# A fused retention and feed-forward kernel: one block of keys-values, one load, one store and the fill-in products of TensorE are moved or reshaped

## The chip, the cores and the metric

The kernel runs on one core of a Trainium2 chip. A core has five engines with instruction streams of their own: TensorE (in profiles PE for its products and PEld for its weight loads), VectorE (DVE), ScalarE (ACT), GpSimd (POOL) and SyncE (SP, which here issues nearly all DMAs). They meet at semaphores. The metric is the device time of one execution in microseconds; before the change it is 181.31 us, the median of three runs (181.07 to 181.83).

## The reference

Two parts follow one another. The first is retention over 4 batches, 8 heads, 768 tokens and head dimension 64: a state of 64 x 64 decays by a factor of its head, takes up the outer product of key and value, and is read by the query. The second is a feed-forward part over the 3072 x 512 result: two products with 512 x 1024 weights, multiplied with each other, then `w3` (1024 x 1024) and `w_out` (1024 x 512).

```
state = gamma * state + outer(k[t], v[t])
y[t]  = q[t] @ state / sqrt(64)
x     = y, heads side by side            # 3072 x 512
out   = ((x @ w1) * (x @ w2)) @ w3 @ w_out
```

Inputs and output are fp32.

## The kernel before

The tokens are worked in 12 steps of 256 (three per batch). Products run in fp16 with fp32 sums. `w3 @ w_out` is multiplied once, in the first 33 us, into eight tiles `W3O`, so that each step needs only three large products.

A step `n` has these parts. Queries, keys and values are loaded (`load`, line 82, or `fetch`, line 120, which is a load by name), cast to fp16 (`cast`, line 314; `cast_v`, line 331, also multiplies the values by a table of decays) and turned: queries and keys go head dimension first, for step 2 and 3 on TensorE (`turn`, line 361, with `turned`, line 374, as the copy out of the accumulator), from step 4 on by a transposing DMA (`dma_turn`, line 354). `scores` (line 390) multiplies keys by queries and `mask` (line 413) masks them on VectorE. `kv` (line 433) multiplies keys by values in small products of 64 rows, and `state` (line 466) adds them up, chunk by chunk, on VectorE (the last multiplication by the decay goes to GpSimd). `inter` and `av` (lines 498 and 534) bring query times state and scores times values into one accumulator, and `x_out` (line 556) writes the step's fp16 activations.

The feed-forward part of a step is four units `u`, each with a block `a` (with `w1`) and a block `b` (with `w2`). A block is eight products of 128 x 128 weights by 256 columns into one bank of the accumulator memory (`two_blocks`, line 578; `blk`, line 704). `evac` (line 707) takes it out: `a` by ScalarE as a copy, `b` by VectorE as the product with that copy. Then `o_unit` (line 636) multiplies with `W3O`, `o_copy` (line 660) copies to an output tile, and `o_store_all` (line 677) stores 512 KB.

The accumulator memory has eight banks, by name: `S0`, `S1`, `X0`, `X1`, `K`, `F0`, `F1`, `F2`. A bank is given again to its next user only when all work on the one before has ended; this holds also where TensorE follows TensorE. Blocks rotate over the three `F` banks.

The order of every engine's work is written out by hand (`tc.manual_schedule`, line 53): the list of calls from line 713 on is the order in which each engine gets its instructions. SyncE's list is in this order too, so a DMA that has to wait for its source holds up those behind it. Loads take a tile of a pool of 18 (`NSTAGE`, line 38).

`warm` (line 688) multiplies zeros into a bank that nobody reads. It is called between the first parts of the work, up to line 771, 18 products of 512 columns in all. Lines 987 to 1000 are what the change touches in step 3: `kv(3, ...)`, the copies and the states around the blocks of step 2. Lines 1001 to 1019 are the loads and turns of the steps 5 to 7. Line 1083 stores the outputs of step 2 (the third), whose tile comes from a rotation of three (`o_tile`, line 651). `YS` (line 197) is a table of decays for steps 0 and 1, last read by `x_out` at line 564. Lines 1178 to 1181 begin the blocks of step 6. Lines 1333 to 1335 are stores near the end.

Of the kernel before, what the change touches and what calls it, by code (L numbers as in the profile page):

```python
# [9 lines left out]
FP = mybir.dt.float32  # L10
# [10 lines left out]
def kernel(  # L21
# [11 lines left out]
    nc = tc.nc  # L33
    B, H, S, D = q.shape
    T = 256
# [5 lines left out]
    DM = 512  # L41
# [4 lines left out]
    const = ctx.enter_context(tc.tile_pool(name="const", bufs=1))  # L46
# [24 lines left out]
    def bank(tag, shape, dtype=FP):  # L71
        return psum.tile(shape, dtype, tag=tag, name="ps" + tag)
# [47 lines left out]
    def fetch(names, via=nc.sync):  # L120
        for x in names.split():
            kind, i = x[:-1], int(x[-1])
            if kind == "r":
                w3_st[i] = load_rows(moe_w3, i, via)
            elif kind == "wo":
                wo_st[i] = load_wo(i, via)
            elif kind in ("w1", "w2"):
                w_st[kind, i] = load_rows({"w1": moe_w1, "w2": moe_w2}[kind], i, via)
            else:
                load(kind, i)  # L130
# [302 lines left out]
    def kv(n, tags, parts=(0, 1)):  # L433
        last = n % PER == PER - 1
        assert kv_n.get(n, 0) == parts[0]
        kv_n[n] = parts[-1] + 1
        if 0 not in parts:
            pass
        elif n < EO:
            KB[n] = [bank(tags[g], [128, NP, 64]) for g in range(2)]  # L440
        else:
            KB[n] = [bank(tags[g], [128, 2, NP, 64]) for g in range(2)]
        for a in range(2 * parts[0], 2 * parts[-1] + 2):
            for t in range(2):
                for g, r in QUARTERS:
                    h = 2 * a + r
                    hd = slice(h * D, (h + 1) * D)
                    if n < EO:
                        o = KB[n][g][half(r), a, :]
                    elif last and (t, g) == (1, 1):  # L450
                        continue
                    else:
                        o = KB[n][g][half(r), t, a, :]
                    nc.tensor.matmul(
                        o, lhsT=k16[n][half(g), t, hd], rhs=v16[n][half(g), t, hd],
                        start=(a == 0 and t == 0), stop=(t == 1), skip_group_check=True,
                    )
# [117 lines left out]

    HT, pa, ht_n = {}, {}, {}

    def two_blocks(W, n, u, tag):
        need(*[(w, d, c) for w in ("w1", "w2") for d in range(4) for c in (0, 512)])
        assert x_n[n] == 2  # L580
        ps = bank(tag, [128, 2, T])
        for i in range(2):
            f = 2 * u + i
            for d in range(4):
                nc.tensor.matmul(  # L585
                    ps[:, i, :], lhsT=W[d][:, f * 128 : (f + 1) * 128], rhs=XT[n][:, d, :],
                    start=(i == 0 and d == 0), stop=(i == 1 and d == 3),
                )
        return ps

    def a_evac(n, u, ps, eng="s"):
# [57 lines left out]
    o_sb, o_n = {}, {}  # L649

    def o_tile(n, tb):
        if n < 2:
            if (n, tb) not in o_sb:
                o_sb[n, tb] = wpool.tile([128, DM], FP, tag=f"wo_{2 * n + tb}", name="osw")
            return o_sb[n, tb][:, :]
        if n not in o_sb:
            o_sb[n] = fsb.tile([128, 2, DM], FP, tag="osb", name="osb", bufs=3)
        return o_sb[n][:, tb, :]
# [26 lines left out]
            o_copy(n, tb, *c)  # L685
            o_store(n, tb, *c)

    def warm(m, tag="X1", w=512):
        ps = bank(tag, [128, 512])
        for _ in range(m):  # L690
            nc.tensor.matmul(ps[:, 0:w], lhsT=zeros[:, 0:128], rhs=zeros[:, 0:w], start=True, stop=True)

    def cast_w(W, st, d, eng, c0=0, c1=DFF):
        done.update((st, d, c) for c in range(c0, c1, 512))
# [6 lines left out]
    ab = {}  # L701
    cuts = ((0, 320), (320, 512))

    def blk(w, n, u, tag):
        ab[w, n, u] = two_blocks(W1 if w == "a" else W2, n, u, tag)

    def evac(w, n, u, eng="s"):
        if w == "a":
            a_evac(n, u, ab.pop((w, n, u)), eng)
        else:  # L710
            b_evac(n, u, ab.pop((w, n, u)))
# [33 lines left out]
    fetch("q3")  # L745
    identity()
    fetch("q4")
    warm(8)
    numbers()
    arguments()  # L750
    tables(4)
# [2 lines left out]
    tables(2)  # L754
    cast_w3(4, "v")
    turn_w3(4, "S0")
    warm(3, "F2")
    turned_w3(4, "v")
    step_decays()
    warm(2, "F2")  # L760
    cast_wo(0, "s")
    cast_w3(1, "v")
    keeps()
    warm(1, "F2")
    cast_w3(2, "gs")
    warm(1, "F2")
    turn_w3(1, "S1")
    tables(0)
    fetch("v3")
    turned_w3(1, "sv")  # L770
    warm(3, "F2")
    cast_wo(1, "g")
    turn_w3(2, "X0")
    w3_mm(1, 0, "S1", first=True)
# [209 lines left out]
    cast_v(4, "g")  # L984
    evac("a", 2, 0)
    blk("b", 2, 0, "F1")
    kv(3, ("X0", "K"))
    turned("q", 3, "v")
    state(3, 1)
    fetch("k5")  # L990
    fetch("v5")
    blk("b", 2, 1, "F0")
    state(3, 2)
    blk("a", 2, 1, "F2")
    state(3, 3)
    scores(3, ("S0", "S1"))
    o_copy(1, 1)
    evac("b", 2, 0)
    state(3, 4)
    state(3, 5)  # L1000
    fetch("k6")
    blk("a", 2, 2, "F1")
    fetch("q6")
    cast("q", 5, "g")
    evac("a", 2, 1)
    evac("b", 2, 1)
# [6 lines left out]
    blk("b", 2, 3, "F1")  # L1013
    inter(3, 0, ("X0", "X1"))
    dma_turn("q", 5)
    fetch("v6")
    mask(3, 0)
    fetch("k7")
# [61 lines left out]
    mask(5, 1)  # L1080
    load("k", 8)
    load("q", 8)
    o_store_all(2)
    o_unit(3, 0, ("F2",))
    o_copy(3, 0)
    o_unit(3, 1, ("F0",))
# [88 lines left out]
    o_copy(5, 0)  # L1175
    o_unit(5, 1, ("F0",), pieces=2)
    o_copy(5, 1)
    blk("a", 6, 0, "F2")
    evac("a", 6, 0)
    blk("b", 6, 0, "F0")  # L1180
    evac("b", 6, 0)
    blk("a", 6, 1, "F1")
    evac("a", 6, 1)
# [147 lines left out]
    x_out(10, 0)  # L1331
    x_out(10, 1)
    o_store_all(8)
    o_store(0, 0)
    o_store(0, 1)
    state(11, 1)
# [92 lines left out]
```

## Time and profile before

| | |
|---|---|
| median of three runs | 181.31 us (181.07 to 181.83) |
| the profiled execution | 181.6 us, span 179.9 us |
| TensorE clock granted, mean | 0.999 |
| TensorE busy | 173.4 us, 96% of the span |
| VectorE, ScalarE, GpSimd busy | 103.0, 66.1 and 63.6 us |
| DMA | 40.22 MB, mean 224 GB/s |
| the products of the blocks (L585) | 640 of 256 columns, 273 ns each from start to end |
| a store of 512 KB, issue to landing | 5.4 us (median) |

The span runs from the first to the last instruction. The duration of one product is from its start to its modelled end; products follow one another much closer than that. The page divides the span in 40 slices of about 4.5 us and gives tenths of busy time for each. The chain that ended last goes back from the last instruction to what released it, or to the instruction before it on the same engine. In rows of the order of time, the columns are start, length (both us), engine, line, operation, tiles written and read, shapes, and how many instructions were merged; square brackets hold the idle time before it and what ended it. The rows of waits give the engine, tile and line that waited, what it waited for, and us in total, times, and the longest.

### The profile page before, as it was taken

The numbers are of one execution on the slowest core, as the hardware profiler recorded it, in microseconds if no ns is written. First come the engines' busy times: TensorE is split into PE (matmuls) and PEld (weight loads), VectorE is DVE, ScalarE is ACT, GpSimd is POOL, SyncE is SP. The second block draws the span as 40 slices with busy tenths as digits, with TensorE's granted clock in tenths as the row PEclk, the third lists the DMA queues.
The fourth block names the chain that finished last, engine by engine and source line by source line (L and its number), as shares of the span: only waits on it lengthen the run. The fifth ranks groups of instructions, "written<-read, shape, count | busy, mean of one in ns | idle before, by whom it ended". The sixth has DMA issues, their size and how long they took to land.

```text
span 179.9 us, 6072 instructions
## 1 busy us (share of the span) xinstructions
PE 173.4 (96%) x2642; PEld 125.7 (70%) x2642; DVE 103.0 (57%) x177; ACT 66.1 (37%) x118; POOL 63.6 (35%) x93
## 2 busy tenths in 40 slices
PE   7989899999999999999999999999999999999993
PEld 2445456688956785885867898768688587786872
DVE  2342789883946487547366384474764946734330
ACT  5436537681238332323314314223222131232422
POOL 7753076446232742724445055250453200000000
PEclk9999999999999999999999999999999999999999
DMA  5999999999899899999999999999999552150303
GB/s 206 409 418 360 357 325 389 408 282 226 181 244 236 204 179 221 202 204 238 178 241 228 237 284 178 212 240 232 271 211 263 170 166 71 70 166 5 117 0 117
DMA packets 80025, 40.22 MB, mean 224 GB/s; under 512 B 59392, under 2 KB 73984, under 8 KB 80000
## 3 DMA queue, kind: packets, MB, share of 16 engines
q1 hardware_dynamic: 79856, 39.33, 88.6%
q8 instruction: 20, 0.33, 0.8%
q10 hardware_dynamic: 144, 0.52, 0.8%
q14 instruction: 5, 0.04, 0.1%
HBM read 29.36 MB, written 6.29 MB: 198 GB/s over the span
## 4 chain that ended last, share of the span: by engine, by line
PE 72%; DMA 15%; SPq 5%; POOL 3%; ACT 2%; DVE 1%; issue 1%; POOLq 0%; DVEq 0%
PE psF L585 38%; PE psF L643 20%; DMA st<-in_v_dram 8%; DMA st<-in_q_dram 4%; DMA st<-in_moe_w_dram 4%; SPq L112 3%; PE psX L521 2%; POOL v L69 2%; PE psX L548 2%; PE psS L406 1%; PE psK L299 1%; PE psF L299 1%; ACT pa L61 1%; SPq L89 1%; PE psF L621 1%; PE psX L621 1%
## 5 line engine op out<-in xcount | busy, mean ns | idle before, releaser
L585 PE MATMUL psF<-xt,w 128*128 128x256 f16 x640 | 71.9, 273 | 0.0
L585 PEld LDWEIGHTS <-w 128*128 128x128 f16 x640 | 62.4, 98 | 9.2
L69 DVE TENSOR_TENSOR ht<-pa,psF 128x512 f16<-128x512 f32 x43 | 29.4, 687 | 38.9 <-PE psF L585 38.8
L61 ACT COPY pa<-psF 128x512 f32<-128x512 f32 x43 | 25.2, 585 | 51.2 <-PE psF L585 45.6
L643 PE MATMUL psF<-w3o,ht 128*128 128x512 f16 (+3 forms) x200 | 38.4, 346 | 0.0
L643 PEld LDWEIGHTS <-ht 128*128 128x128 f16 x224 | 20.7, 98 | 17.5
L69 POOL TENSOR_TENSOR v<-st,VN 128x1024 f16<-128x1024 f32 x10 | 19.0, 1902 | 37.2 <-DMA st<-in_v_dram 18.5
L663 ACT ACTIVATE osb<-psF 128x512 f32<-128x512 f32 (+2 forms) x18 | 9.9, 550 | 31.0 <-PE psF L643 31.0
L566 DVE TENSOR_TENSOR xt<-psX,YN 128x512 f16<-128x512 f32 x19 | 12.8, 724 | 5.7 <-PE psX L548 5.7
L426 DVE TENSOR_TENSOR am<-psS,keep 128x512 f16<-128x512 f32 x19 | 12.5, 681 | 2.6 <-PE psF L406 2.6
L621 PEld LDWEIGHTS <-w 128*128 128x128 f16 x128 | 12.1, 98 | 2.4 <-issue 0.5
L61 POOL CAST q<-st 128x1024 f16<-128x1024 f32 x10 | 10.4, 1039 | 7.2 <-DMA st<-in_q_dram 4.3
L61 POOL CAST k<-st 128x1024 f16<-128x1024 f32 x9 | 9.3, 1036 | 6.2 <-PE psX L548 3.1
L299 PEld LDWEIGHTS <-w3t 128*128 128x128 f16 x64 | 5.8, 98 | 6.4 <-issue 0.7
L621 PE MATMUL psF<-xt,w 128*128 128x256 f16 x56 | 9.7, 272 | 0.0
L69 POOL TENSOR_TENSOR t<-s,GS 128x256 f16<-128x256 f32 x8 | 5.8, 727 | 11.0 <-DVE s L69 11.0
L521 PE MATMUL psX<-qT,t 64*64 64x64 f16 (+1 forms) x296 | 7.6, 199 | 0.0
L69 POOL TENSOR_TENSOR v<-st,VS 128x1024 f16<-128x1024 f32 x2 | 3.9, 1932 | 8.9 <-DMA st<-in_v_dram 8.9
L521 PEld LDWEIGHTS <-t 64*64 64x64 f16 x320 | 4.9, 106 | 3.0 <-issue 2.5
L69 DVE TENSOR_TENSOR t<-psK,t 128x256 f16<-128x256 f32 x15 | 6.2, 415 | 0.4
L283 PEld LDWEIGHTS <-w3h 128*128 128x128 f16 x64 | 4.2, 101 | 2.9 <-DVE w3h L61 1.4
L621 PE MATMUL psX<-xt,w 128*128 128x256 f16 x32 | 6.1, 273 | 0.1
(127 smaller groups left out, 192.4 us busy)
## 6 DMA issues: line engine op xcount, KB each, us to landing
st<-in_moe_w_dram SPq DMA_DIRECT2D x15, 512.0 KB, 8.7
st<-in_k_dram SPq DMA_DIRECT2D x20, 256.0 KB, 5.7
st<-in_q_dram SPq DMA_DIRECT2D x10, 512.0 KB, 6.1
st<-in_v_dram SPq DMA_DIRECT2D x20, 256.0 KB, 4.6
out_dram<-osb SPq DMA_DIRECT2D x9, 512.0 KB, 5.4
st<-in_moe_w_out_dram SPq DMA_DIRECT2D x4, 512.0 KB, 9.8
st<-in_k_dram SPq DMA_DIRECT2D x2, 512.0 KB, 6.5
st<-in_q_dram SPq DMA_DIRECT2D x8, 128.0 KB, 6.5
```

Of the source, the lines that this page charges most:

```text
L61: {"v": nc.vector.tensor_copy, "g": nc.gpsimd.tensor_copy, "s": nc.scalar.copy}[eng](dst, src)
L69: (nc.vector if eng == "v" else nc.gpsimd).tensor_tensor(dst, a, b, op)
L112: via.dma_start(t[:, :].rearrange("p (t n) -> p t n", t=2), moe_w_out[i * 256 : (i + 1) * 256, :].rearrange("(p t) n -> p t n", t=2),)
L283: nc.tensor.transpose(ps[:, g * 128 : (g + 1) * 128], src[:, c0 : c0 + 255 : 2], ident16[:, :])
L299: nc.tensor.matmul(acc[f][:, :], lhsT=w3t[f][:, g * 128 : (g + 1) * 128], rhs=WO[i][:, r, :], start=(first and r == 0), stop=(last and r = ...
L426: nc.vector.tensor_tensor(t[:, :, :, :].rearrange("p a s i -> p (a s) i"), ps[:, :, :, :].rearrange("p a s i -> p (a s) i"), keep64[:, :]. ...
L521: nc.tensor.matmul(dst, lhsT=TS[n, c][half(r), a, :], rhs=rhs, start=((g, o) not in begun), stop=False, skip_group_check=True,)
L566: nc.vector.tensor_tensor(XT[n][:, :, :].rearrange("p a (s x) -> p (a s) x", s=2)[:, :, g * 64 : (g + 1) * 64].rearrange("p k (i t) -> p k ...
L585: nc.tensor.matmul(ps[:, i, :], lhsT=W[d][:, f * 128 : (f + 1) * 128], rhs=XT[n][:, d, :], start=(i == 0 and d == 0), stop=(i == 1 and d = ...
L621: nc.tensor.matmul(rows_ps[w, n, uh][j // 2][:, j % 2, :], lhsT=W[d][:, f * 128 : (f + 1) * 128], rhs=XT[n][:, d, :], start=(first and j % ...
L643: nc.tensor.matmul(ps[:, x : x + w], lhsT=HT[n][:, f, tb * 128 : (tb + 1) * 128], rhs=W3O[f][:, c0 + x : c0 + x + w], start=(f == 0 and x ...
L663: nc.scalar.activation(dst, src, AF.Copy, scale=final_scale)
```

## The change

It has five parts.

- In step 3, `kv(3)` and the first `state` after it come behind block `b` of unit 1 rather than ahead of it, and the `evac` of block `b` of unit 0 comes ahead of the states.
- The load of the queries of step 6 is issued behind the two turns of step 5 rather than ahead of them.
- The outputs of step 2 go to a tile of their own, in the place of the table `YS`, and are stored near the end, behind the outputs of step 8.
- The products of zeros read the same zeros as fp32: eleven of 256 or 128 columns for 18 of 512. Each is one instruction of the program, where the fp16 ones were a weight load and a product.
- The blocks `a` and `b` of unit 0 in step 6 are multiplied in pieces of 128 columns: 32 products for 16.

```
-    def two_blocks(W, n, u, tag):
+    def two_blocks(W, n, u, tag, pieces=1):
...
             for d in range(4):
-                nc.tensor.matmul(
-                    ps[:, i, :], lhsT=W[d][:, f * 128 : (f + 1) * 128], rhs=XT[n][:, d, :],
-                    start=(i == 0 and d == 0), stop=(i == 1 and d == 3),
-                )
+                for x in range(0, T, T // pieces):
+                    nc.tensor.matmul(
+                        ps[:, i, x : x + T // pieces], lhsT=W[d][:, f * 128 : (f + 1) * 128],
+                        rhs=XT[n][:, d, x : x + T // pieces], start=(i == 0 and d == 0 and x == 0),
+                        stop=(i == 1 and d == 3), skip_group_check=pieces > 1,
+                    )
...
+        if n == 2 and n not in o_sb:
+            o_sb[n] = const.tile([128, 2, DM], FP, tag="YS", name="osy")
...
-    def warm(m, tag="X1", w=512):
-        ps = bank(tag, [128, 512])
+    def warm(m, tag="X1", w=256):
+        ps, z = bank(tag, [128, 512]), zeros[:, :].bitcast(FP)
         for _ in range(m):
-            nc.tensor.matmul(ps[:, 0:w], lhsT=zeros[:, 0:128], rhs=zeros[:, 0:w], start=True, stop=True)
+            nc.tensor.matmul(ps[:, 0:w], lhsT=z[:, 0:128], rhs=z[:, 0:w], start=True, stop=True)
...
-    warm(8)
+    warm(4)
...
     turn_w3(4, "S0")
-    warm(3, "F2")
+    warm(1, "F2")
+    warm(1, "F2", w=128)
     turned_w3(4, "v")
     step_decays()
-    warm(2, "F2")
+    warm(1, "F2")
     cast_wo(0, "s")
     cast_w3(1, "v")
     keeps()
-    warm(1, "F2")
+    warm(1, "F2", w=128)
     cast_w3(2, "gs")
-    warm(1, "F2")
+    warm(1, "F2", w=128)
     turn_w3(1, "S1")
     tables(0)
     fetch("v3")
     turned_w3(1, "sv")
-    warm(3, "F2")
+    warm(1, "F2")
+    warm(1, "F2", w=128)
...
     blk("b", 2, 0, "F1")
-    kv(3, ("X0", "K"))
     turned("q", 3, "v")
-    state(3, 1)
     fetch("k5")
     fetch("v5")
     blk("b", 2, 1, "F0")
+    kv(3, ("X0", "K"))
+    evac("b", 2, 0)
+    state(3, 1)
     state(3, 2)
     blk("a", 2, 1, "F2")
     state(3, 3)
     scores(3, ("S0", "S1"))
     o_copy(1, 1)
-    evac("b", 2, 0)
     state(3, 4)
     state(3, 5)
     fetch("k6")
     blk("a", 2, 2, "F1")
-    fetch("q6")
...
     dma_turn("q", 5)
+    fetch("q6")
     fetch("v6")
...
-    o_store_all(2)
...
-    blk("a", 6, 0, "F2")
+    blk("a", 6, 0, "F2", pieces=2)
     evac("a", 6, 0)
-    blk("b", 6, 0, "F0")
+    blk("b", 6, 0, "F0", pieces=2)
...
     o_store_all(8)
+    o_store_all(2)
     o_store(0, 0)
```

More of the change, by code (lines that the diff above doesn't have):

```diff
@@ L702, with blk @@
     cuts = ((0, 320), (320, 512))
-    def blk(w, n, u, tag):
-        ab[w, n, u] = two_blocks(W1 if w == "a" else W2, n, u, tag)
+    def blk(w, n, u, tag, pieces=1):
+        ab[w, n, u] = two_blocks(W1 if w == "a" else W2, n, u, tag, pieces)
     def evac(w, n, u, eng="s"):
```

## The prediction

> **What bounds the kernel now.** I read the page's first two parts, then the waits of TensorE, the order of time on the engines around those waits, the chain that ended last, and SyncE's queue.
>
> ```profile
> span 179.9 us, 6072 instructions
> PE 173.4 (96%) x2642; PEld 125.7 (70%) x2642; DVE 103.0 (57%) x177; ACT 66.1 (37%) x118; POOL 63.6 (35%) x93
> PE   7989899999999999999999999999999999999993
> DMA  5999999999899899999999999999999552150303
> ```
>
> TensorE is busy throughout, with the DMA engines loaded beside it until slice 32. The execution took 181.6 us, 1.7 more than its span and 0.3 above the median of the three runs (181.31); I work out the difference in this execution and take it off the median.
>
> ```profile
> PE psX L691 <- DVE zeros L136: 1.3, 1, 1.3
> PE psS L299 <- DVE w3t L61: 0.6, 1, 0.6
> PE psX L370 <- DVE q L61: 0.6, 1, 0.6
> PE psX L454 <- POOL v L69: 0.3, 1, 0.3
> ```
>
> These are nearly all of TensorE's idle waits. The first three lie in the first 23 us. Only the last comes later, and it is the one that the moved keys-values touch. The order of time on TensorE and, behind the dots, on GpSimd:
>
> ```profile
> 59.36 1.91 PE L585 MATMUL psF<-xt,w 128*128 128x256 f16 x16
> 61.60 0.19 PE L454 MATMUL psX<-v,k 64*64 64x64 f16 x1 [0.33 <-POOL v L69]
> ...
> 61.97 1.92 PE L585 MATMUL psF<-xt,w 128*128 128x256 f16 x16
> 63.83 0.45 PE L406 MATMUL psS<-qT,kT 64*64 64x64 f16 x32
> ...
> 59.64 3.80 POOL L69 TENSOR_TENSOR v<-st,VN 128x1024 f16<-128x1024 f32 x2 [4.49 <-DMA st<-in_v_dram]
> ```
>
> Sixteen products of L585 (two blocks) from 61.97 are followed by 64-row products at 63.83, 1.86 later, undisturbed. The sixteen from 59.36 should so have been followed at 61.22; the keys-values (L454) began at 61.60. They waited 0.38 us for the first of two value casts, which ran from 59.64 to about 61.55 because its load had landed at 59.48 only. After 62 TensorE has no wait left that the profile names.
>
> ```profile
> 107.84 6.99 PE psF L585 x64
> 119.54 6.99 PE psF L585 x64
> 131.31 6.99 PE psF L585 x64
> 143.20 6.99 PE psF L585 x64
> ```
>
> These lines of the chain give the later steps: 11.70, 11.77 and 11.89 us from one step's blocks to the next one's, and 6.99/64 = 109 ns for a product of 256 columns, where its streaming sets the pace. Beyond 62 us only instructions taken off TensorE, or a hiccup like that of the third interval, can shorten the end.
>
> **The change, part by part.**
>
> Keys-values of step 3 behind block b1. TensorE takes the eight products of b1 (8 x 0.109 = 0.87 us) in the place of the wait, from 61.11 (59.36 + 16 x 0.109). b1 needs its bank F0 back from ScalarE's copy of a0, which ran from 60.43 to 61.01: 0.10 us to spare. The keys-values then start at about 62.1, with their values ready at 61.55: 0.5 us of cover. The number of changes between 128-row and 64-row products stays. Gain 0.38 us. From values 0.5 us later than now the gain shrinks, and at 0.9 it is gone.
>
> What queues behind: step 3's states on VectorE read the keys-values, and start at 62.7 where they started at 62.09. The product b0, which stood behind three of them (63.42), is moved ahead, to about 61.3, when TensorE has finished it; so bank F1 is free at 62.0 for a2, now due about 63.9. The states end near 64.4, as before (64.44), b1's product follows, and F0 is free near 65.1 for a3, due 65.7. GpSimd's multiplication of the last state (64.51) stays. So I find no new wait here; each of these has 0.6 us or more.
>
> Queries of step 6 behind the turns. SyncE's queue now:
>
> ```profile
> 69.83 2.75 SPq L94 DMA_DIRECT2D st<-in_q_dram  x1
> 72.69 2.06 SPq L357 DMA_TRANSPOSE kT<-k  x1
> 74.86 2.33 SPq L357 DMA_TRANSPOSE qT<-q  x1
> ```
>
> The load took 2.75 us of the queue. Without it the turn of the keys could be issued at 69.8, but its source is cast on GpSimd from 69.28 to 70.32, so it goes at 70.35, 2.3 us earlier, and the turn of the queries with it. By the page's medians to landing (6.1 and 3.9 us) the two landed near 78.8 by estimate; step 5's scores came around 79.8, without a wait. The path gains nothing by 2.3 us more slack, yet the 0.38 us saved above eat a third of the old slack of 1.0, so this keeps it safe. The load itself is issued some 5 us later (74.9), and lands near 80 to 82; its cast on GpSimd (77.66) moves behind it, to 82 at most, and the cast of step 6's values, at 82.61, stands next. The queries of step 6 are turned from 85.78, some 3 us after. Loads of values and keys behind it on the queue find the same number of bytes ahead of them. Cost on the path 0; if the cast came after 82.61 it would push the value cast and the key cast of step 7 by 1 us, with scores at 91 still 5 us off.
>
> Third outputs stored late. One store of 512 KB leaves the queue at 91.89 (2.38 us of SyncE) and goes in at 144.4, where the DMA row falls to 5, 5, 2. Their own buffer is the early table YS, last read near 37 us. The turn of step 7's keys goes out up to 2.4 us earlier; nobody on the path waits for it. At the end the last outputs are issued at 175.7 to 177.2, 30 us behind this store. The other outputs keep three buffers, and each is still reused three steps later. 0 on both sides; if the DMA were still full at 144, 512 KB at the 224 GB/s of the page are 2.3 us, which still ends 25 us before the last store.
>
> Two blocks in pieces. Sixteen products of 256 columns become 32 of 128. Eight turns of 128 columns, each with its own weight load, take 0.45 us (51.11 to 51.56), 56 ns each. 32 x 56 - 16 x 109 = +0.05 us on TensorE's path. Between ends: +0.04, what the pieces of step 5's outputs (32 products in 3.60 us where others have 16 in 3.56) cost, and +1.4, had each to wait out its weight load (32 x 98 ns - 1.75). The turns are the nearer row, since there the loads hide: +0.05.
>
> Zero products in fp32. Before, 18 of 512 columns fill TensorE's waits in the first 8.7 us:
>
> ```profile
> 4.78 0.83 PE L283 MATMUL psS<-ident,w3h 128*128 128x128 f16 x8
> 5.44 2.32 PE L691 MATMUL psF<-zeros 128*128 128x512 f16 x7
> 7.61 0.62 PE L283 MATMUL psS<-ident,w3h 128*128 128x128 f16 x8
> 8.06 0.81 PE L691 MATMUL psF<-zeros 128*128 128x512 f16 x3
> 8.96 0.62 PE L283 MATMUL psX<-ident,w3h 128*128 128x128 f16 x8
> 10.20 1.02 PE L299 MATMUL psS<-wo,w3t 128*128 128x512 f16 x4 [0.62 <-DVE w3t L61]
> ```
>
> After, eleven, of 256 and 128 columns. No fp32 product is in this trace. If one streams its columns four times, 256 of them take what two old products took, and 128 what one took: the total is then the same, 18 units. Each new group in bank F2 waits for the one before (the old ones start 0.22 us late at 6.31, 6.96 and 7.39), and there are two more such waits, one before each turn: about 0.25 us, so the third turn moves from 8.96 to 9.2. Its copy on VectorE cannot start before 10.06 (9.72 + 0.42, less overlap) and then finds its source ready at 9.8: nothing is passed on. Bounds: once through (a quarter of the time) would free 2 us that the first turn (waiting for a cast until 4.73) and the loads take back, 0; every one of 44 passes behind a whole weight load of 98 ns adds 4.3 us. What may be late for nothing is 0.5 (that copy), 0.3 (its product at 11.05, ready at 10.74), 0.2 (a wait at 13.15) and 0.6 (the wait for queries at 22.59), 1.6 us, of which 0.25 are used. Past 1.35 us, 30 ns per pass, every further us is one on the end. I take 0, because streaming hides the loads in every row of 128 columns here.
>
> The Trainium skill, "TensorE: Matmul & The Clock Gate", speaks against this edit: by its section on weight-path modes, weights of 128 columns load fast unless they are fp32, and by its section on LDWEIGHTS a plain load takes columns/1.2 ns, 107 ns here. Taken at its word, passes of 256 columns (107 ns warm) just hide that and the sixteen of 128 columns would stand behind it for about 50 ns each, an estimate of 0.8 us, inside the 1.35; the sum would not move, and no run here shows an fp32 load.
>
> Sum: -0.38 + 0.05 + 0 + 0 + 0 = -0.33 us, in this execution 181.27, and off the median 181.0.
>
> **The rivals.**
>
> No gain: the wait comes back elsewhere. For it: bank F0 is free only 0.10 us before b1 needs it, value loads land late everywhere in this stretch, and step 5's turns have 1 us. Against it: each has its own cover, above. With the 0.38 lost: 181.4.
>
> Slower: fp32 weight loads stand open. Place: the eleven zero products, before the third turn. Price: 44 passes x 98 ns = 4.3, less 1.35 hidden, +3.0, and with the rest 184.0; it decides from 38 ns per pass, where 44 x 38 - 1350 ns eat the 0.33 gained. For it: no such row here, and weight loads of fp32 are twice the bytes. Against it: all fp16 loads hide.
>
> The instruction stream shifts. Zero products take 25 rows fewer from the head, pieces put 32 more in at step 6 (+7 after it). The third interval above is 0.12 to 0.19 longer than others with nothing that TensorE waits for by the profile. If it is an accident of where the queue stands, it can go (180.8) or come in one more step (181.2).
>
> Faster beyond that: 180.2 would need 0.8 us more than the only late wait holds, and I see no row to take it from but the first 40 us, where TensorE's waits for VectorE are not touched.
>
> **How the numbers follow.** The forecast 0.50, no gain 0.17, the stream's shift 0.12, slower by weight loads 0.13, faster beyond 0.08. The range from 180.4 to 181.9 holds the first three with the spread of the runs (181.07 to 181.83) around them, and leaves out most of the last two. A measurement tells about 0.5% from no change: 180.40 and 182.22. Faster 0.10 (the last case and an edge of the third), same 0.75, slower 0.15 (weight loads, and a little for a wait that I missed).
>
> **What would show it.** After: TensorE's wait for the value cast at L454 is gone, sixteen plus eight blocks' products run through 61 us, and keys-values start near 62.1; the step intervals stay at 11.7 to 11.9, with step 6's 0.05 longer; turns of step 5 are issued near 70.3 and 72.5, ahead of the load; the store of the third outputs stands near 144; the zero products end at about 8.9 and the waits before 10.20 and 22.59 are still there, only shorter. A wait before 22.59 that is gone, or a start of L370 after 22.6, would make the prediction wrong towards slower; a new wait of L585 for ScalarE at 61.1 or of L406 for a turn at 79.5 towards no change.

## The result, and the profile after

The changed kernel takes 182.31 us (median of 22 runs, 181.14 to 183.96), the kernel before, run beside it, 181.18 us (22 runs, 180.76 to 182.64). The ratio is 1.006, with a 95% interval of 1.0039 to 1.0081: slower by 0.6%, some 1.1 us, where 181.0 and no change were forecast, and outside the forecast range of 180.4 to 181.9. The ratios here are of undisturbed runs, while the medians count every run, so the two need not agree to the last digit. The profiled execution took 182.08 us with a span of 180.3, against 181.6 with 179.9 before. So this pair of traces holds 0.4 to 0.5 of the 1.1 us: the profiled run before is 0.4 us above its kernel's median and that of the changed kernel 0.2 below its own, and many other runs of the changed kernel must lose more than the profiled one did.

The head of the page of the changed kernel:

```profile
span 180.3 us, 6112 instructions
PE 174.2 (97%) x2662; PEld 128.1 (71%) x2662; DVE 103.3 (57%) x177; ACT 66.2 (37%) x118; POOL 63.4 (35%) x93
PE   7999899999999999999999999999999998999993
DMA  5999999999999999999999999899999583150303
q8 instruction: 21, 0.34, 0.9%
```

TensorE has 20 more products than the 2642 before, and the queue that carries instructions has one packet more than before:

```profile
q8 instruction: 20, 0.33, 0.8%
```

The waits of TensorE in the changed kernel (total, times, longest, in us):

```profile
PE psX L695 <- DVE zeros L136: 1.3, 1, 1.3
PE psX L548 <- issue: 0.7, 1, 0.7
PE psX L370 <- DVE q L61: 0.6, 1, 0.6
```

The wait for the value cast at L454 is gone, as forecast. In its place stands one that the forecast did not have: "issue", which means that TensorE waited for nothing that the profile shows. The chain that ended last (start, length) tells when:

```profile
59.43 2.62 PE psF L586 x24
62.05 0.14 PE psX L454
...
107.34 7.03 PE psF L586 x80
...
119.09 6.99 PE psF L586 x64
...
127.30 3.68 PE psF L645 x16
130.98 6.99 PE psF L586 x64
...
142.70 6.99 PE psF L586 x64
...
150.57 0.20 PE psX L548 x21
150.77 0.74 issue
151.51 0.28 PE psX L548 x9
151.78 3.56 PE psF L645 x16
155.34 6.99 PE psF L586 x64
```

Against the starts shown before the change (107.84, 119.54, 131.31, 143.20) the blocks of the later steps now start 0.50, 0.45, 0.33 and 0.50 us earlier. That is the forecast gain, and some 0.1 us of the head with it. It is lost at one place, 150.77, in the middle of the 64-row products of L548: the next step's blocks start at 155.34, 0.43 later than in the chain before:

```profile
154.91 6.99 PE psF L585 x64
```

A smaller loss of the same kind is in the line 127.30, where sixteen products take 3.68 us that elsewhere take 3.56.

### The profile page after: what moved, and what is told of

Same layout as the page of the kernel before. It is cut to its first block, busy times and chain, and to the rows that moved or that the text cites. A ratio compares the mean times of both kernels' runs of the same rounds, so it can differ in the third digit from the quotient of the medians.

```text
span 180.3 us, 6112 instructions
## 1 busy us (share of the span) xinstructions
PE 174.2 (97%) x2662; PEld 128.1 (71%) x2662; DVE 103.3 (57%) x177; ACT 66.2 (37%) x118; POOL 63.4 (35%) x93
## 4 chain that ended last, share of the span: by engine, by line
PE 85%; DMA 7%; SPq 4%; DVE 1%; issue 1%; ACT 0%; DVEq 0%
PE psF L586 39%; PE psF L645 21%; DMA st<-in_q_dram 4%; DMA st<-in_moe_w_dram 4%; PE psF L623 3%; SPq L112 3%; PE psX L521 2%; PE psX L623 2%; PE psX L548 2%; PE psX L645 2%; PE psS L406 2%; PE psS L623 2%; PE psK L299 1%; PE psF L299 1%; SPq L89 1%; PE psK L645 1%
## 5 line engine op out<-in xcount | busy, mean ns | idle before, releaser
L586 PE MATMUL psF<-xt,w 128*128 128x256 f16 (+1 forms) x656 | 71.9, 270 | 0.0
L667 ACT ACTIVATE osb<-psF 128x512 f32<-128x512 f32 (+2 forms) x16 | 8.7, 544 | 28.2 <-PE psF L645 28.2
L299 PEld LDWEIGHTS <-w3t 128*128 128x128 f16 x64 | 5.7, 98 | 5.8 <-DVE w3t L61 0.6
L623 PE MATMUL psF<-xt,w 128*128 128x256 f16 x56 | 9.7, 272 | 0.0
L548 PE MATMUL psX<-am,v 64*64 64x64 f16 (+1 forms) x336 | 6.1, 197 | 0.7 <-issue 0.7
```

The source lines that it names most:

```text
L299: nc.tensor.matmul(acc[f][:, :], lhsT=w3t[f][:, g * 128 : (g + 1) * 128], rhs=WO[i][:, r, :], start=(first and r == 0), stop=(last and r = ...
L548: nc.tensor.matmul(o, lhsT=v16[n][half(g), t, h * D : (h + 1) * D], rhs=rhs, start=((g, c) not in begun), stop=(n >= EO or t == 1), skip_g ...
L586: nc.tensor.matmul(ps[:, i, x : x + T // pieces], lhsT=W[d][:, f * 128 : (f + 1) * 128], rhs=XT[n][:, d, x : x + T // pieces], start=(i == ...
L623: nc.tensor.matmul(rows_ps[w, n, uh][j // 2][:, j % 2, :], lhsT=W[d][:, f * 128 : (f + 1) * 128], rhs=XT[n][:, d, :], start=(first and j % ...
L667: nc.scalar.activation(dst, src, AF.Copy, scale=final_scale)
```

## Where the time goes: blocks of TensorE's instructions

TensorE's instructions come into the core as packets of 16,384 bytes on queue 8, the line "q8 instruction" above. I call an instruction a row; a product and its weight load are two rows, and the gaps below, a multiple of 256 rows apart, show that a packet holds 256. Every product stands in the trace in order, so the rows at any moment can be counted from it: counted from 1, the k-th product's load is row 2k - 1 and the product row 2k, apart from the few rows of other instructions. The table has the places behind 55 us in all traces where TensorE idles by 0.1 us or more over its usual pace with no wait for anybody, at the first row of a block:

```
kernel             gap at (us)   over usual (us)   row    = 187 + 256 x   packet of the block sent / ended
changed            128.54        0.11              4027   15              126.27 / 127.59
changed            150.58        0.90              4795   18              149.17 / 150.05
e1_no_pieces        93.45        0.50              2747   10               91.33 /  92.64
e3_moves_only      152.69        0.40              4795   18              150.93 / 151.81
e4_store_early      93.28        0.15              2747   10               90.93 /  92.03
e4_store_early     150.88        1.37              4795   18              149.88 / 150.76
e5_plus24           91.77        1.06              2746   10 (less 1)      90.25 /  91.35
e5_plus24          131.29        0.45              4026   15 (less 1)     129.30 / 130.46
e9_store_later     131.80        1.07              4027   15              130.45 / 131.49
e12_fp32_even       94.80        0.52              2747   10               93.06 /  94.06
e13_all_even       152.83        0.80              4795   18              151.44 / 152.32
e16_plus56         127.61        0.98              4026   15 (less 1)     126.02 / 126.95
```

The traces of the kernel before and of the other eight experiments have none at such a row. Idle places of 0.11 to 0.15 us that are not at such a row stand in seven traces (before, e4, e8, e9, e14, e15 and e16), all between 137.9 and 140.5 us, and are left unexplained. The row fits to one instruction. In nine of the twelve gaps the weight load is late and the product with it; in the three of e5 and e16 the load comes on time and only the product is late, so the block begins one row sooner there ("less 1"), and the traces of these two have one more semaphore instruction on TensorE, between 59 and 60 us, than the others in the table. So behind 55 us every idle place of 0.2 us or more that no wait explains falls on the first row of a new block of 256. In all twelve TensorE goes on 1.3 to 1.7 us after that block's packet has ended. And the packet is sent only near the time when TensorE enters the block ahead of it: in the changed kernel at 90.48 for an entry at 90.80, at 126.27 for 126.07, at 149.17 for 147.67. From the entry into one block until the next is used there are 2.4 to 4.7 us in these cases, once 6.7. Over all 270 blocks behind 55 us in the 18 traces, none is used sooner than 1.28 us after its packet's end; the packet is sent from 1.6 us before to 4.2 us after that entry, eight in ten times between 0.35 before and 2.87 after. Most blocks last much longer than that (11.07 us where a step's 256-column products fill them). But a step also has about 120 products of 64 rows, which take 1.2 us together, and a block that holds most of those 240 rows needs only 1.3 to 3.5 us.

Which rows share a block depends on how many rows come before. From the trace before, counted with the rows moved by s, the shortest blocks behind 55 us last:

```
rows added    shortest blocks: us (at us)
 0            3.52 (91), 3.54 (150), 4.12 (111)
 8            2.69 (91), 2.88 (150)
24            1.31 (91), 2.11 (149)
32            1.71 (91), 2.51 (149)
40            2.11 (90), 2.69 (127), 2.92 (148)
56            1.31 (126), 2.90 (89), 2.91 (68)
-8            3.71 (112), 4.35 (91), 4.35 (150)
```

The change adds rows twice. The eleven fp32 products of zeros, each one instruction of the program, show in the trace as 22 pairs of load and product, 44 rows for the 36 of the eighteen old ones: 8 more from the head on. The two blocks in pieces add 16 products: 40 more from step 6 on (107 us). Both gaps of the changed kernel lie in blocks that the table has as short with 40 rows. They come to 1.01 us; without them its profiled run of 182.08 would be at 181.07, where 181.0 was forecast. This count was made after the result; the experiments test it.

## The experiments

**First: which part costs the time?** Four kernels each take something out of the changed kernel. Beside them the kernel before took 181.25 us (35 runs).

e1 leaves step 6's blocks whole, so 8 rows stay added throughout:

```diff
-    blk("a", 6, 0, "F2", pieces=2)
+    blk("a", 6, 0, "F2")
...
-    blk("b", 6, 0, "F0", pieces=2)
+    blk("b", 6, 0, "F0")
```

> The changed kernel with the two blocks of step 6 whole again, all else as changed. In its trace TensorE's instruction stream stands still twice with no wait: after row 4026 (0.11 us at 128.7) and after row 4794 (0.90 us at 150.6), 768 rows or three blocks of 256 apart, and the page counts 21 instruction packets of 16 KB (20 before). Theory A, the place of the code in these blocks: without the pieces the rows from step 6 on stand 8 rather than 40 later than before the change. Blocks of rows that begin near 91 and 150 us then last 2.7 and 2.9 us by the old trace (3.5 before), so the gap at 150.6 moves to about 153 and a gap near 94 may come; time between 180.8 and 182.0, fewer runs above 183. Theory B, the late store crowds the DMA engines at 150: nothing changes, 182.3. Theory C, the pieces cost by themselves: only their 0.04 us goes, 182.2.

Measured: 181.82 us (181.16 to 183.25), 1.0036 [1.0011, 1.006]. The gap at 150 is gone from its trace, but one of 0.50 us stands at 93.45, where 8 rows make a block of 2.69 us.

e2 takes the old fp16 zero products instead (32 rows from step 6 on):

```diff
-    def warm(m, tag="X1", w=256):
-        ps, z = bank(tag, [128, 512]), zeros[:, :].bitcast(FP)
+    def warm(m, tag="X1", w=512):
+        ps = bank(tag, [128, 512])
...
-    warm(4)
+    warm(8)
...
```

> The changed kernel with the zero products as before (18 of 512 columns in fp16), pieces and all moves kept. The trace of the changed kernel shows the eleven fp32 products as 22 pairs of a weight load and a product, so they add 8 rows to the head. Theory A: rows stand as before up to step 6 and 32 later from there; the block that begins near 149 lasts 2.5 us by the old trace, shorter than the 2.9 of the changed kernel, so the gap there stays or grows: 182.0 to 183.0. Theory B: no change, 182.3. Theory C, the fp32 products cost by themselves: back to 181.0 or below.

Measured: 181.62 us (181.24 to 186.42), 1.0023 [1.0004, 1.0042], less than the 182.0 to 183.0 expected from the rows, and no gap in the one trace. The packet that had to come while the short block near 148 ran was sent 0.62 us before the entry there: a short block alone makes no gap where its packet is early.

e3 has neither added part, only the three moves, and so the old rows:

```diff
-    warm(4)
+    warm(8)
...
-    blk("a", 6, 0, "F2", pieces=2)
+    blk("a", 6, 0, "F2")
...
-    blk("b", 6, 0, "F0", pieces=2)
+    blk("b", 6, 0, "F0")
```

> Keys-values, load and store moved as in the change; zero products and blocks as before. No row is added. Theory A: no block of 256 rows lasts less than 3.5 us, as before the change; only the 0.38 us of the keys-values' wait go: 180.8, and the spread of the runs is that of before. Theory B, the late store alone: 182.0 or more, with a gap near 150. Theory C, added instructions cost by themselves: 180.8 too, so this run does not tell A from C.

Measured: 181.72 us (181.18 to 183.1), 1.0025 [1.0003, 1.0046]. That was a surprise: with no row added it is still not as fast as the kernel before. Its trace has a gap of 0.40 us at 152.69, where the packet was sent 1.56 us after the entry.

e4 puts the store of the third outputs back to its old place:

```diff
+    o_store_all(2)
     o_unit(3, 0, ("F2",))
...
     o_store_all(8)
-    o_store_all(2)
```

> The changed kernel with the store of the third outputs at its old place. Theory A: the rows stand as in the changed kernel, so the stream still has to wait near 150.6; with 512 KB less on the DMA engines at 144 to 148 the packet may come sooner, 181.5 to 182.3. Theory B, the store is the cause: the gap at 150.6 goes and the time is 181.0 or less. Theory C: 182.3.

Measured: 182.07 us (181.38 to 184.75), 1.0048 [1.0016, 1.0079], with 1.37 us lost at the same row 4795:

```profile
PE psX L548 <- issue: 1.2, 1, 1.2
```

So the late store is not needed for that gap, since it is there without it. Neither of the added parts alone seems to be the whole loss: e1, e2 and e3 are all between 1.002 and 1.004, and the changed kernel is 1.006, though the intervals of all four overlap.

**Second: rows and nothing else.** These two kernels are the kernel before, but with more and narrower zero products in its first call: the same columns (20 x 205 = 4100 and 36 x 114 = 4104, for 8 x 512 = 4096), in 24 and 56 rows more. No product behind the head is changed, no DMA is moved.

```diff
-    warm(8)
+    warm(20, w=205)
```

> The kernel before, with one edit: the first eight zero products of 512 columns are twenty of 205 columns, the same columns in all, so that every later row of TensorE stands 24 rows later. In five traces every gap of TensorE that no wait explains stood ahead of a row 187 + 256 k (2747, 4027, 4795), 1.3 to 1.5 us after a 16 KB packet on the instruction queue had ended, and from the entry of one block to the first row of the next there were 2.8 to 4.3 us. Theory A (the blocks): by the old trace the block that is entered near 91 us is used up in 1.3 us and that near 149 in 2.1, so gaps of 1.5 to 3 us near 92 and 0.7 to 2.2 near 151 must come, ahead of rows 187 + 256 k: 183.3 to 186. Theory B (the moves make the loss): 181.2 as before, since nothing is moved.

Measured: 183.88 us (182.37 to 186.83, 6 runs), 1.0105 [1.0052, 1.0157], beside 181.26 (28 runs) for the kernel before. In its trace TensorE waits as follows, and loses most of the time in the block that the table has as 1.31 us long at 91 (timeline: start, length):

```profile
PE psX L548 <- issue: 0.9, 1, 0.9
...
PE psF L643 <- issue: 0.3, 1, 0.3
```

```profile
91.50 0.46 PE L548 MATMUL psX<-am,v 64*64 64x64 f16 x30
92.85 0.22 PE L548 MATMUL psX<-am,v 64*64 64x64 f16 x2 [0.89 <-issue]
```

The gaps are shorter than expected (1.06 us there, for 1.5 to 3). A second one was expected near 151 and is not in this trace: that packet was sent 1.35 us ahead of the entry. The one at 131.29 was not expected; its packet was sent 2.05 us after the entry.

The same line with 56 rows should have the place at 126 instead:

```diff
-    warm(8)
+    warm(36, w=114)
```

> The kernel before with the first eight zero products as 36 of 114 columns: every later row 56 rows later, nothing else. Theory A: by the old trace the block entered near 126 us is used up in 1.3 us (in the run with 24 rows more it was the one at 91), so the gap must stand near 127 to 128, ahead of row 4027, 1.5 to 3 us long, and smaller ones may come near 92 and 71 (2.9 us each): 182.7 to 184.5. If the number of small products itself cost, the loss would stand in the head, before 23 us.

Measured: 184.13 us (182.66 to 187.9, 6 runs), 1.0136 [1.0103, 1.017], beside 181.13 (29 runs). The gap has moved to where the count puts it:

```profile
127.35 0.46 PE L548 MATMUL psX<-am,v 64*64 64x64 f16 x30
128.62 0.22 PE L548 MATMUL psX<-am,v 64*64 64x64 f16 x2 [0.81 <-issue]
```

Two kernels with the same work and other row counts, each slower by over 1% and each with its longest gap in the block forecast as the shortest: that settles that rows alone can cost more than this whole change does. In both, the products on either side of that gap belong to L548, and the profile shows no wait between them. Nor do the added zero products cost this time in the head: in e16's trace the blocks start 0.07 us later than before at 107.91 and at 119.61, and 1.09 later at 132.40, behind the gap.

e6 goes the other way. It leaves out four zero products, which feed nothing, for 8 rows fewer:

```diff
-    warm(1, "F2")
...
-    warm(3, "F2")
```

> The kernel before without four of its zero products (one of them ahead of, three behind the second turn of the third weights): every later row stands 8 rows earlier. Theory A: the shortest block of rows lasts 3.7 us (near 112) instead of 3.5 (near 91 and 150), and those two 4.35: no gaps, or rarer ones; 181.0 with less spread upwards. Theory B: 181.2. If the lost zero products cost something in the head (the clock closes, a turn comes later), 181.5 or more, and a granted clock below 1 before 15 us.

Measured: 181.28 us (180.36 to 182.16), 0.9985 [0.9964, 1.0007]: unclear. Its times fall into two groups, five from 180.36 to 180.82 and seven from 181.27 to 182.16, and its trace (180.82) is of the first; what makes the second is not known.

**Third: the parts one by one.** e7 is the kernel before with the keys-values' move alone:

```diff
-    kv(3, ("X0", "K"))
     turned("q", 3, "v")
-    state(3, 1)
     fetch("k5")
     fetch("v5")
     blk("b", 2, 1, "F0")
+    kv(3, ("X0", "K"))
+    evac("b", 2, 0)
+    state(3, 1)
...
-    evac("b", 2, 0)
```

> The kernel before with the keys-values of step 3 (and their first state, and the product of block b of unit 0) moved, alone. No row moves by more than a block of the feed-forward part near 62 us. My prediction: 0.38 us less, 180.8 to 180.9. Theory A: TensorE comes 0.38 us earlier to each of the two blocks that last 3.5 us, the packets are sent when the block is entered and wait behind loads, so part of it may be given back as gaps near 94 and 153: 180.8 to 181.2. Theory B: 180.8.

Measured: 180.92 us (180.69 to 181.35), 0.997 [0.9947, 0.9993], the narrowest spread of all twelve-run kernels, beside 181.26. The difference of the medians is 0.34 us. The span of the trace and the blocks that now run through:

```profile
span 179.2 us, 6072 instructions
```

```profile
59.25 2.78 PE L585 MATMUL psF<-xt,w 128*128 128x256 f16 x24
```

e8 is the kernel before with the late store alone:

```diff
+        if n == 2 and n not in o_sb:
+            o_sb[n] = const.tile([128, 2, DM], FP, tag="YS", name="osy")
...
-    o_store_all(2)
     o_unit(3, 0, ("F2",))
...
     o_store_all(8)
+    o_store_all(2)
```

> The kernel before with the store of the third outputs moved to the end, alone. My prediction: no change, 181.2. Theory A: the packet entered near 150 stands behind 512 KB more that are issued at 144.5; in the run with all moves it was sent 1.56 us after the block was entered, in the old trace 0.77 before: a gap near 153 in many runs, 181.3 to 181.8. Theory B (the store makes the loss): 181.7.

Measured: 181.69 us (180.97 to 183.16), 1.003 [1.0004, 1.0056]. The store that was costed at nothing costs about 0.3% here. Its trace, of a run of 181.23 us, shows no gap at a block's start, so the cause isn't seen in it.

e10 is e7 and the load behind the turns:

```diff
-    fetch("q6")
     cast("q", 5, "g")
...
     dma_turn("q", 5)
+    fetch("q6")
```

> Keys-values and load moved, store, zero products and blocks as before. The keys-values alone gave 180.92. My prediction: the load's place costs nothing, 180.9. If the turns 2 to 3 us earlier help instruction packets or anything else, 180.7; if the later queries hurt, 181.2 or more and GpSimd waits for them behind 80 us.

Measured: 181.34 us (180.84 to 182.77), 1.0003 [0.998, 1.0026], beside 181.27 (35 runs). Against e7 it is 0.3% worse with intervals that overlap: whether the load's place costs something is not settled. Its trace has no gap at a block's start.

**Fourth: the added parts with their rows made even.** If rows are what the pieces and the fp32 products cost, they should be free when as many rows are taken off. e11 is e10 with step 6's pieces, and with the outputs of step 5, which were in pieces, whole: 32 rows less just ahead of 32 more.

```diff
-    o_unit(5, 0, ("F2",), pieces=2)
+    o_unit(5, 0, ("F2",))
...
-    o_unit(5, 1, ("F0",), pieces=2)
+    o_unit(5, 1, ("F0",))
...
-    blk("a", 6, 0, "F2")
+    blk("a", 6, 0, "F2", pieces=2)
...
-    blk("b", 6, 0, "F0")
+    blk("b", 6, 0, "F0", pieces=2)
```

> Keys-values and load moved, the blocks of step 6 in pieces, and in return the outputs of step 5 whole: 32 rows fewer at step 5 and 32 more just behind, so that from block b of step 6 on every row stands where it stood before the change, with the pieces done. Theory A (only the place counts): as the run without pieces, 180.9, no gap near 127 or 151. Theory C (pieces cost by themselves): 181.4 or more.

Measured: 180.99 us (180.67 to 182.25), 0.9988 [0.9969, 1.0008]. With the rows made even the pieces cost nothing that these runs can show.

e12 is e7 with nine fp32 zero products in the place of eleven, 18 pairs and 36 rows as in the kernel before:

```diff
-    def warm(m, tag="X1", w=512):
-        ps = bank(tag, [128, 512])
+    def warm(m, tag="X1", w=256):
+        ps, z = bank(tag, [128, 512]), zeros[:, :].bitcast(FP)
...
-    warm(8)
+    warm(4)
...
-    warm(3, "F2")
+    warm(1, "F2")
...
-    warm(2, "F2")
+    warm(1, "F2")
...
```

> Keys-values moved, and the zero products as nine in fp32, which are 18 pairs of a weight load and a product in the trace of the changed kernel, as many rows as the 18 in fp16 had; nothing else. Theory A: 180.9, as the keys-values alone, and the 22.5 us at which the turn of the queries begins stay. Theory C (fp32 products cost by themselves): 181.4 or more, with a later start of that turn or a later clock.

Measured: 181.28 us (180.76 to 182.65), 1.0014 [0.9989, 1.0038]. Seven runs are at 180.76 to 181.32, like e7, and five at 182.06 or more. The trace is of one of the five (182.21): a gap of 0.52 at row 2747, and this wait, with the turn of step 5's queries behind the load as in the old order, and TensorE 0.25 us earlier at step 5's products than before the change (79.27 for 79.52):

```profile
PE psS L406 <- DMA qT<-q: 0.2, 1, 0.2
```

So fp32 itself need not be on the path (seven runs are as fast as e7; the loss of the other five is seen in one trace only), and the second part of the change, the load behind the turns, guards against a wait that the first part can bring about.

e13 is the changed kernel, with all five parts, and the rows of both added parts made even:

```diff
     warm(1, "F2")
-    warm(1, "F2", w=128)
...
-    warm(1, "F2", w=128)
...
-    o_unit(5, 0, ("F2",), pieces=2)
+    o_unit(5, 0, ("F2",))
...
-    o_unit(5, 1, ("F0",), pieces=2)
+    o_unit(5, 1, ("F0",))
```

> All five parts of the change, with its rows made even: nine fp32 zero products (36 rows, as before) rather than eleven, and the outputs of step 5 whole, which takes off the 32 rows that the pieces of step 6 add. Theory A (the place of the rows): the loss by rows goes, what stays is the late store's: as the moves alone, 181.5 to 181.7, no gap at 127, one near 153 at times. Theory C (fp32 products, pieces or all parts together cost by themselves): 182.0 or more.

Measured: 181.6 us (181.19 to 184.01), 1.0026 [1.0013, 1.004], where the changed kernel had 1.0060 [1.0039, 1.0081]. The loss is more than halved by making the rows even, with intervals that only just touch. Its trace still has a gap, at a block that lasts 3.5 us, where the packet was sent 1.92 us after the entry:

```profile
150.66 2.55 PE L645 MATMUL psF<-w3o,ht 128*128 128x512 f16 x11
153.85 1.25 PE L645 MATMUL psF<-w3o,ht 128*128 128x512 f16 x5 [0.64 <-issue]
```

**Fifth: the store, once more.** In e3 and e13 the packet that came late was near 150, some us after the stores at 144. e9 is e3, and e14 is e13, each with the store of the third outputs behind the next pair of stores, where the queue has it at 157 to 158:

```diff
     o_store_all(8)
-    o_store_all(2)
...
+    o_store_all(2)
```

> All three moves, zero products and blocks as before (no row added), but the late store goes behind the stores near 157 us and not those near 144. Moves alone gave 181.72 with a gap of 0.40 us at 153 ahead of row 4795, whose packet was sent 1.56 us after its block was entered. Theory A (instruction packets, held up by the 512 KB at 144 to 150): the gap and the loss go, since the next packet after 157 has ten us to spare: 180.9 to 181.1. Theory B, that the store costs wherever it is late (its buffer, the queue): 181.6 or more.

> As the run with all five parts and rows even, and the late store behind those near 157 us. Theory A: 181.0 to 181.3, between the moves with the store at 157 (181.37) and the keys-values alone (180.92). If the place of the store does not matter: as with the store near 144.

Measured: e9 181.37 us (181.03 to 182.2), 1.0008 [0.9989, 1.0026], where e3 had 1.0025; e14 181.27 us (180.8 to 182.39), 1.0021 [1.0004, 1.0038], where e13 had 1.0026. The medians fall by 0.35 and 0.33 us, but the intervals overlap. For e9 that lies between the 180.9 to 181.1 expected if the store held up packets and the 181.6 if it cost wherever it is late. No gap at 150 in either trace; e9's has one of 1.07 us at 131.80, far from the store. With e8 this makes it likely that a store near 144 costs time. That it does so by holding up the packet near 150 is argued, not shown: of the six traces with the store near 144, three have that packet sent 1.5 us or more after the entry (changed, e3, e13) and three ahead of it (e1, e2, e8), and of the twelve without that store one has it 1.90 after (e4).

e15 joins e7 and e6, the keys-values' move and 8 rows fewer (the same four zero products left out):

```diff
-    warm(1, "F2")
...
-    warm(3, "F2")
...
-    kv(3, ("X0", "K"))
...
     blk("b", 2, 1, "F0")
+    kv(3, ("X0", "K"))
```

> Keys-values moved, and four zero products fewer, so that all later rows stand 8 rows earlier (shortest block 3.7 us near 112, others 4.35 or more). Theory A: the gain of the keys-values and fewer gaps, 180.5 to 180.9. If fewer zero products cost in the head: 181.0 or more. The first run with these four left out alone had a lowest time of 180.36 and a median of 181.28, so both are open.

Measured: 180.71 us (180.33 to 182.36), 0.9981 [0.9956, 1.0007] beside 181.13. It is the lowest median here, 0.2% less than e7's, and with this spread not clear of no change. Of all kernels only e7 is clear of the kernel before on the faster side.

## Why the prediction was wrong

What held. The keys-values' wait is gone and the 0.38 us arrived: the blocks are 0.50 us ahead at 107.34, 0.1 of it from the head, and e7 alone gains 0.3% (0.34 us by the medians). The pieces were given +0.05 us: their line of the chain reads 7.03 us where whole blocks have 6.99. The turns were expected at 70.3 and 72.5, ahead of a load at 74.9. SyncE's queue in the changed kernel:

```profile
69.89 3.40 SPq L357 DMA_TRANSPOSE kT<-k  x1
73.40 1.24 SPq L357 DMA_TRANSPOSE qT<-q  x1
74.70 1.39 SPq L94 DMA_DIRECT2D st<-in_q_dram  x1
```

The fp32 zeros were given 0 on the path. TensorE's order of time in the head of the changed kernel:

```profile
5.40 3.04 PE L695 MATMUL psF<-zeros 128*128 128x256 f32 x10
8.28 0.61 PE L283 MATMUL psS<-ident,w3h 128*128 128x128 f16 x8
8.73 1.20 PE L695 MATMUL psF<-zeros 128*128 128x256 f32 x4
9.76 0.61 PE L283 MATMUL psX<-ident,w3h 128*128 128x128 f16 x8
10.21 1.03 PE L299 MATMUL psS<-wo,w3t 128*128 128x512 f16 x4
```

The third turn is later than the forecast 9.2 (9.76, before 8.96), but the products of L299 begin at 10.21 where they began at 10.20, and the queries' wait at L370 ends at 22.52 after 22.59. The wait of 0.62 us before L299 took most of it and is gone, though it was forecast to be only shorter. The rest went on: the copy of the third turn began at 10.41, not at the forecast 10.06, and the products that read it at 11.16 for 11.05, before the wait at 13.15 took that too. So the 0 came out by the slack that the prediction had counted, and not by its reason that streaming hides the loads: the passes of 128 columns came 0.21 us apart, and a load took 0.19. The weight loads themselves, by the group of that line:

```profile
L695 PEld LDWEIGHTS psF<-zeros x14: 186/189/192, 5.3 to 9.5; 128*128 128x128 f32 x14
L695 PE MATMUL psF<-zeros x14: 275/377/483, 5.4 to 9.7; 128*128 128x128 f32 x8, 128*128 128x256 f32 x6
```

That is a median of 189 ns for an fp32 load, against 98 for fp16 before. The Trainium skill, "TensorE: Matmul & The Clock Gate", section "Weight-path perf modes", has it that fp32 weights do not load fast, and the trace agrees (189 against 98). The plain load of 107 ns that the prediction worked out from the section on LDWEIGHTS of the same page of the Trainium skill is too low for these: 186 to 192 were measured. The rival that put its chance on these loads had the price of one too small (98 ns), but twice too many of them: 22 loads show and not 44.

What failed. The step is the shift of the instruction stream, which the sum put at nothing; in the changed kernel's trace it costs 1.01 us. The rival "the instruction stream shifts" named the cause, but its count was wrong and so was its size. It reckoned 25 rows fewer from the head and 7 more after step 6; measured are 8 more and 40 more, because an fp32 product, counted as one row, shows as two loads and two products, four rows. And its price of 0.12 to 0.19 us came from a hiccup in the old trace that does not lie at a block's start; a gap at a block's start costs 0.1 to 1.4 us in these traces, and there can be two in a run. Nothing in the sum stood for it, though SyncE's and GpSimd's queues were each followed. The old trace had what was needed: the count of packets on queue 8, the rows of the products, and two blocks of 3.5 us that were already near the edge. At 94.84 the kernel before enters a block whose packet had ended 1.83 us earlier, when the gaps above end 1.3 to 1.7 us behind theirs.

The second step that failed is the late store, "0 on both sides". Alone it costs 0.3% (e8). I had asked when its bytes leave and who waits for its buffer, but not what else is on the DMA queues after 144, and the profile lists the instruction packets among them. Whether they are what it delays stays open.

By the ratios: e7 stands at 0.997 and the changed kernel at 1.006, 0.9% to explain. By the middle values, making the rows even takes 0.34% of it off (1.006 to 1.0026, e13), the late store alone is 0.3% (e8), and the load's place 0.33% by e10 against e7, which isn't clear of nothing. These are differences of ratios whose intervals are some 0.2% wide to either side, and the parts need not add up, since the same gap can be made by a short block and a late packet together. e14, with all parts, even rows and the store at 157, is still 1.0021 [1.0004, 1.0038]: some of the loss of 0.5% against e7 remains without a name. What decides from run to run whether a packet is early (0.94 us ahead of the entry in e8 near 150) or late (1.92 us behind it in e13) is open, and so is whether it can be steered other than by the row count.

The Trainium skill, "Runtime: NRT & Kernel Launch", section "Instruction fetch mechanics", speaks of instructions in 16 KiB blocks of 256, the next fetched while the current one runs, at a cost that is mostly hidden. The traces agree on the packets and on the distance of 256 rows between gaps. They disagree on the last for this kernel: 0.90 us open at 150.58 in the changed kernel, 1.37 in e4.

## What to carry to other kernels

Count rows as well as time: in a kernel that keeps TensorE full, an edit that changes the number of its instructions moves every later block of 256, and where a block falls on a run of short products (here 240 rows in 1.2 us) the next block may not be there yet. When a trace shows an idle "issue" in the middle of a group, count the instructions from the start and see whether it falls on a multiple of 256 past the others. Measure a cosmetic edit, such as zero products in other widths, with as much care as a real one, and where it can be done keep the row count (e13 more than halved the loss that way, but did not remove it).

## What was not expected of the hardware

- In these traces TensorE's instructions come one block of 256 ahead and no more (sent from 1.6 us before to 4.2 us after the entry into the block ahead), their packet takes 0.88 to 1.46 us in 95 of 100 cases (2.96 at most), and in the gaps TensorE goes on 1.3 to 1.7 us after its end: a packet sent a microsecond later can show on the path.
- Of the two passes of an fp32 product, one of 256 columns took some 0.43 us in the first 4 us, as much as a 512-column fp16 product there; later the second pass of 256 columns came 0.27 to 0.32 us after the first, that of 128 columns 0.21.
- Products of 64 rows with their own loads went at some 10 ns each (120 in 1.17 us), so that 256 rows are used up in 1.4 us (e5: 2.48 us, 1.06 of them the gap; e16: 2.40 with 0.98). From the start of a packet to the first use of its block there were at least 2.3 us.
- The same work with 24 and 56 rows more in the head took 1.05% and 1.36% longer.
